# Loads of y and of the token-block tasks on GpSimd's queue, and other turns for the second pair's tasks

## The chip, the cores and the metric

The kernel runs on 1 core of one Trainium2 chip. The metric is device time in microseconds (us) of one execution; the time given for a kernel is the median of its runs. All tensors are float32. Matrix products are made from float32r operands (a float32 value split in a high and a low part, `split` below), three products for each pair of operands (`mm3`).

Engines by the profile's names: PE is TensorE (matmuls), DVE is VectorE, ACT is ScalarE, POOL is GpSimd, SP is SyncE, which here only issues DMA transfers. SPq and POOLq are the instruction queues of SP and GpSimd. Each engine works through its own list of instructions in order and stands at an instruction until the semaphores that it waits for have come; what is behind it in the list waits too.

## The reference

`x` is 2048 tokens of 640 features. It is normalized, and three things are added up: `x`, the real part of a two-dimensional discrete Fourier transform of the normalized `x`, and a gated MLP of it.

```python
def _A_ref(x, dft_seq_re, dft_seq_im, dft_hid_re, dft_hid_im):
    a = jnp.einsum("bsd,ed->bse", x, dft_hid_re)
    b = jnp.einsum("bsd,ed->bse", x, dft_hid_im)
    return jnp.einsum("ts,bse->bte", dft_seq_re, a) - jnp.einsum("ts,bse->bte", dft_seq_im, b)

def _B_ref(x, W_gate, W_up, W_down):
    gate = jnp.einsum("bsd,df->bsf", x, W_gate)
    up = jnp.einsum("bsd,df->bsf", x, W_up)
    gate = gate * (gate > 0)
    return jnp.einsum("bsf,fd->bsd", gate * up, W_down)

xn = _layernorm(x, axis=-1)
return x + _A_ref(xn, ...) + _B_ref(xn, ...)
```

The sizes: S = 2048 tokens, D = 640, F = 1728. The products are made in a Strassen-like scheme (blocks B11, B12, B21, B22 and their sums T1 to T4), so sums of blocks are prepared on VectorE ahead of the matmuls.

## The kernel before

**Two phases.** Phase 1 makes the Fourier part. It works on four chunks `c` of 512 token columns (CH). For each chunk, tiles of the sequence DFT matrices (128 x 1024, 512 KB) are loaded (L482, L564: `raw` and `tk`), combined on VectorE (L560), split by ScalarE (L105) and VectorE (L106) into a ring of three tiles `cb`, and multiplied with the normalized tokens. `raw` has five buffers, and a load that needs one waits until VectorE has finished with it. Then five `hidden` units for each half m = 1 and m = 0 multiply by the hidden DFT (weights `in_hid`, loaded in L657, split into `wu`), and their result is added to `y` (L671). The two `y` buffers hold 5 x 512 columns each; a chunk's y is loaded from the transposed x in `hidden`'s `load` (L655, the residual `x`), and, for chunks 0 and 1, stored to the DRAM tensor `y_early` one unit after the last addition (L674, GpSimd). The next chunk's L655 writes the same buffer, so it waits until L674 has landed.

Phase 2 makes the MLP for two pairs of chunks, q = 1 first (chunks 2 and 3), then q = 0. A unit `gate_up(q, f)` (f = 0 to 12, plus a rest) loads and splits gate and up weights (L785, `z`, `gw`) and makes 54 matmuls with ScalarE and VectorE copies between them (L820 `p`, L823 `oa`, L825 `u`, L829, L831, L832, L836, L839, L840), and leaves `h`. After units 1, 3, 5, 7, 9, 11 and 12 a unit `down` multiplies two `h` by W_down (weights L766, `wdt`) and adds to `y` (L910).

**Token-block tasks.** The MLP needs the normalized tokens transposed, in the blocks of the scheme. For each pair q six tasks (`token_sets`, steps 0 to 5) make them: load the rows of mean and reciprocal deviation, broadcast to all partitions (L300 or L317, from `rows`), and a block of the transposed x (L301 or L318, from `in_xt`), into two buffers `st` called `mr` and `a` or `ab`; normalize and combine in place on VectorE (`make`: L304 and L305 for steps 0 and 1; L323, L324 and L327 for steps 2 to 5); store to the DRAM tensor `set` on GpSimd (L307, or two stores in L336). Steps 2 to 5 have four loads each (two L317, two L318), steps 0 and 1 three (two L300, one L301). Each task's loads write the two buffers that the task before has used, so they wait until its stores have landed. The sets are loaded again in L629 (`load_set`, SP) and split into `xs_early` and `sets_b`, the operands of the MLP.

Pair 1's tasks run in phase 1, from chunk 0's V3 on, 14 units or more apart (SPACE): `make` six units after the load, the store eight units after. Pair 0's tasks run in phase 2 while q = 1 is computed: a task is a unit of its own in front of `gate_up(1, f)` for the f in SET_TURNS, its `make` comes one unit and its store two units after the load. At f = 11 the first finished set of pair 0 (B12) is loaded (`load_set_now`); the scheduler puts that load and its copies into the lists as early as it believes the data to be there.

**What sets the order.** The list `todo` holds units with four steps: load, prepare, run, finish. `drive` goes through them with loads four units (phase 1) or two units (phase 2) ahead of the run; `defer` places makes and stores a number of units later. From this the tile framework's scheduler makes one list for each engine. In the kernel before, all loads stand in SP's list: DFT tiles, hid weights, y, rows, in_xt, sets, z, W_down. GpSimd's list has the stores to `first`, `set`, `y_early` and little else.

Of the kernel before, what the change touches and what calls it, by code (L numbers as in the profile page):

```python
# [12 lines left out]
P = 128  # L13
S, D, F = 2048, 640, 1728
KD = D // P
CH = 512
W2 = 2 * CH
HC = CH // 2
# [28 lines left out]
def fnet_reglu_kernel(  # L47
# [15 lines left out]
    nc = tc.nc  # L63
# [31 lines left out]
    def bank():  # L95
        return psum_p.tile([P, CH], F32, name="ps")

    def stage():
        return stages[-1].tile([P, W2], F32, name="st")
# [4 lines left out]
    def split(hi, lo, src):  # L104
        nc.scalar.activation(hi, src, AF.Copy)  # L105
        return nc.vector.tensor_tensor(lo, src, hi.bitcast(F32), op=OP.subtract)  # L106

    def mm3(ps, w, m, first, last, more=False):

        (wh, wl), (mh, ml) = w, m  # L110
        nc.tensor.matmul(ps, wh, mh, start=first, stop=False, skip_group_check=more)  # L111
        nc.tensor.matmul(ps, wh, ml, start=False, stop=False, skip_group_check=more)  # L112
        nc.tensor.matmul(ps, wl, mh, start=False, stop=last, skip_group_check=more)  # L113
# [6 lines left out]
    def defer(units, f):  # L120

        deferred.setdefault(now[0] + units, []).append(f)
# [155 lines left out]
    def token_sets(q, step, stage=stage, distance=(6, 8)):  # L278

        ch = xt[:, q * W2 : (q + 1) * W2].rearrange("(k p) t -> k p t", p=P)  # L280
        st_r = rows[:, q * W2 : (q + 1) * W2]
        tt = nc.vector.tensor_tensor
        part = lambda st, i: st[:, i * CH : (i + 1) * CH]
        t = {}

        def unit(load, make, keep):
            def begin():
                load()
                defer(distance[0], make)
                defer(distance[1], keep)  # L290

            todo.append((begin, idle, idle, idle))

        if step < 2:
            cs = slice(step * CH, (step + 1) * CH)

            def load():
                t["mr"], t["a"] = stage(), stage()[:, :CH]
                for i in range(2):
                    nc.sync.dma_start(part(t["mr"], i), st_r[i : i + 1, cs].to_broadcast([P, CH]))  # L300
                nc.sync.dma_start(t["a"], ch[4][:, cs])  # L301

            def make():
                tc.keep_in_program_order(tt(t["a"], t["a"], part(t["mr"], 0), op=OP.add))  # L304
                tt(t["a"], t["a"], part(t["mr"], 1), op=OP.mult)  # L305

            unit(load, make, lambda: nc.gpsimd.dma_start(sets[q][X4][:, cs], t["a"]))  # L307
            return

        k, hs = (step - 2) // 2, (step - 2) % 2 * HC  # L310
        hs = slice(hs, hs + HC)
        cols = lambda ap: ap.rearrange("p (c t) -> p c t", c=2)

        def load():
            t["mr"], t["ab"] = stage(), stage()
            for i in range(2):
                nc.sync.dma_start(cols(part(t["mr"], i)), cols(st_r[i : i + 1])[:, :, hs].to_broadcast([P, 2, HC]))  # L317
                nc.sync.dma_start(cols(part(t["ab"], i)), cols(ch[k + 2 * i])[:, :, hs])  # L318

        def make():  # L320
            mr, ab = t["mr"], t["ab"]
            for i in range(2):
                tc.keep_in_program_order(tt(part(ab, i), part(ab, i), part(mr, 0), op=OP.add))  # L323
                tt(part(ab, i), part(ab, i), part(mr, 1), op=OP.mult)  # L324

            (a0, a1, b0, b1), (t1, t2, t3, t4) = ([st[:, i * HC : (i + 1) * HC] for i in range(4)] for st in (ab, mr))
            sub = lambda o, i0, i1: tt(o, i0, i1, op=OP.subtract)  # L327
            sub(t1, a1, a0)
            sub(t2, b1, t1)
            sub(t3, b1, a1)  # L330
            sub(t4, b0, t2)

        def keep_sets():
            cs = slice(k * CH + hs.start, k * CH + hs.stop)
            for i, st in ((B11, t["ab"]), (T1, t["mr"])):
                nc.gpsimd.dma_start(sets[q][i : i + 4, :, cs].rearrange("i p t -> p i t"),  # L336
                                  st.rearrange("p (i t) -> p i t", i=4))

        unit(load, make, keep_sets)
# [15 lines left out]
    def raw():  # L355
        return raw_p.tile([P, W2], F32, name="raw")
# [280 lines left out]
    def load_set_now(q, blocks):  # L637
        for i in blocks:
            for step in load_set(q, [i]):
                step()  # L640

    def y_chunk(half, e):
        return Y[half][:, e]

    def hidden(c, m, e):
        t = {}
        half = int(c == NCHUNK - 1)
        y = lambda: y_chunk(half, e)
        first = m == 1

        def load():
            if first:
                if (c, e) == (NCHUNK - 1, 0):
                    Y[1] = get_right()
                nc.sync.dma_start(y(), xt[e * P : (e + 1) * P, c * CH : (c + 1) * CH])  # L655
            t["s"] = raw()[:, :D]
            nc.sync.dma_start(t["s"], hid[m, e])  # L657

        def prepare():
            t["w"] = w = wring.tile([P, 2, D], F32R, name="wu")  # L660
            split(w[:, 0], w[:, 1], t["s"])

        def run():
            ps = bank()
            for i, d in enumerate((0, 1, 4, 2, 3)):
                mm3(ps, (t["w"][:, 0, d * P : (d + 1) * P], t["w"][:, 1, d * P : (d + 1) * P]),
                    PQ[c, m, d], i == 0, i == KD - 1)
            t["ps"] = ps

        def finish():  # L670
            nc.vector.tensor_tensor(y(), t["ps"], y(), op=OP.add)  # L671
            if not first and c < 2:
                b = c * CH
                defer(1, lambda: nc.gpsimd.dma_start(y_early[:, e, b : b + CH], y()))  # L674

        todo.append((load, prepare, run, finish))

    def drive(far, ahead, pinned=None):
# [237 lines left out]
        todo.append((idle, prepare, run, idle))  # L916

    load_set_now(1, SETS_B)
    SET_TURNS = [1, 2, 4, 6, 8, 9]
    for q in (1, 0):  # L920
        gate_up_rest(q)
        fs = [NF]
        for f in range(NF):
            if q == 1 and f in SET_TURNS:
                token_sets(0, SET_TURNS.index(f), lambda: pool("stage3").tile([P, W2], F32, name="st"), (1, 2))
            gate_up(q, f)
# [43 lines left out]
```

## Time and profile before

| what | value |
|---|---|
| median of 3 runs | 1078.13 us (1075.41 to 1082.65) |
| the profiled execution: time | 1079.5 us |
| the profiled execution: span from first to last instruction | 1077.7 us |
| mean granted TensorE clock in it | 0.995 |
| busy ACT / POOL | 402.3 us (37%) / 33.0 us (3%) |
| DMA moved, over the span | 164.52 MB, mean 153 GB/s |
| GpSimd's own transfers (software_dynamic queue) | 19.40 MB, 4.6% of the DMA engines' span |

Transfers that the change and the prediction speak of, from the list of DMA issues: what and where to, who issues, how many, size, median time from issue to landing.

| transfer | queue | count | KB each | us to landing |
|---|---|---|---|---|
| raw<-in_dft | SP | 94 | 512 | 4.3 |
| y<-in_xt (L655) | SP | 20 | 256 | 4.5 |
| st<-rows (L300, L317) | SP | 24 | 256 | 4.7 |
| st<-in_xt (L301, L318) | SP | 20 | 256 | 3.3 |
| st<-set (L629) | SP | 18 | 512 | 3.8 |
| out<-y | SP | 20 | 256 | 3.0 |
| set<-st (L336) | GpSimd | 16 | 512 | 5.6 |
| y_early<-y (L674) | GpSimd | 10 | 256 | 4.1 |

How to read it: the span is covered by the engine that is busy nearly all of it, so the interesting numbers are the places where that engine is idle, and what released it there. A transfer's time to landing counts from its issue to the semaphore of its last byte. A row of waits names the waiting engine and line, what released it, the microseconds in total, how often, and the longest. A row of the chain of waits names a start, a length and the work that the next piece waited for. In a row of the timeline, start and length are followed by engine, line, operation, operands and count; the bracket is idle time before, and what ended it.

### The profile page before, as it was taken

How to read it: one execution, taken by the hardware profiler on the slowest of the kernel's cores; microseconds unless marked ns; L12 is line 12 of the kernel's file. 1: busy time of each engine (PE TensorE's matmuls, PEld its weight loads, DVE VectorE, ACT ScalarE, POOL GpSimd, SP SyncE). 2: the span in 40 equal slices, each digit the busy share in tenths (PEclk: the TensorE clock that was granted, in tenths of full speed). 3: DMA queues.
4: the chain of work that ended last, by engine and by line, in shares of the span. 5: the costliest groups of instructions: out<-in, count | busy, mean ns of one | idle time of the engine just before them, and what ended most of it. 6: DMA issues, size and time to landing. Idle time of an engine off the chain costs nothing.

```text
span 1077.7 us, 12192 instructions
## 1 busy us (share of the span) xinstructions
PE 1059.7 (98%) x4660; PEld 872.1 (81%) x4660; DVE 784.7 (73%) x1085; ACT 402.3 (37%) x506; POOL 33.0 (3%) x51
## 2 busy tenths in 40 slices
PE   8999999999989999999999999999999999999998
PEld 6888888878778887888888888877888888888886
DVE  7946986875689488668588778677569865685654
ACT  5744453432333233344352422322244433233211
POOL 2100000000000000000000000010000000000000
PEclk9999999999999999999999999999999999999999
DMA  8974654666477567435462232343039211111002
GB/s 307 347 249 162 234 176 142 230 227 215 170 236 240 191 213 263 164 122 183 149 200 99 96 127 86 104 138 113 26 112 323 80 59 52 49 50 49 25 1 98
DMA packets 60410, 164.52 MB, mean 153 GB/s; under 512 B 8128, under 2 KB 16320, under 8 KB 60352
## 3 DMA queue, kind: packets, MB, share of 16 engines
q1 hardware_dynamic: 55456, 144.35, 40.8%
q0 software_dynamic: 4896, 19.40, 4.6%
q8 instruction: 36, 0.59, 0.2%
q14 instruction: 22, 0.18, 0.1%
HBM read 139.07 MB, written 23.61 MB: 151 GB/s over the span
## 4 chain that ended last, share of the span: by engine, by line
PE 68%; issue 18%; DVE 7%; DMA 5%; ACT 1%; POOL 0%; SPq 0%; POOLq 0%; DVEq 0%; ACTq 0%
PE ps L111 22%; PE ps L113 22%; PE ps L112 22%; DMA raw<-in_dft 2%; DMA set<-st 1%; DVE cb L106 1%; PE ps L907 1%; DVE y L910 1%; DMA st<-set 1%; DVE raw L560 1%; DMA st<-in_wd 1%; DMA y<-in_x 0%; DVE st L327 0%; DVE st L324 0%; DVE xs_early L106 0%
## 5 line engine op out<-in xcount | busy, mean ns | idle before, releaser
L105 ACT ACTIVATE cb<-raw 128x1024 fp32r<-128x1024 f32 x78 | 82.1, 1056 | 121.6 <-PE ps L113 102.3
L106 DVE TENSOR_TENSOR cb<-raw,cb 128x1024 fp32r<-128x1024 f32 x78 | 94.9, 1220 | 44.5 <-ACT cb L105 41.2
L910 DVE TENSOR_TENSOR y<-ps,y 128x512 f32<-128x512 f32 x140 | 91.1, 687 | 17.5 <-PE ps L113 16.8
L112 PE MATMUL ps<-cb,xs_late 128*128 128x512 f32 x256 | 100.5, 393 | 2.7 <-DVE cb L106 2.7
L112 PE MATMUL ps<-h,wdt 128*128 128x512 f32 x260 | 101.3, 389 | 0.0
L111 PE MATMUL ps<-xs_early,gw 128*128 128x512 f32 x260 | 101.1, 389 | 0.0
L113 PE MATMUL ps<-h,wdt 128*128 128x512 f32 x260 | 101.1, 389 | 0.0
L112 PE MATMUL ps<-xs_early,gw 128*128 128x512 f32 x260 | 101.1, 389 | 0.0
L113 PE MATMUL ps<-xs_early,gw 128*128 128x512 f32 x260 | 101.1, 389 | 0.0
L111 PE MATMUL ps<-h,wdt 128*128 128x512 f32 x260 | 100.3, 390 | 0.0
L111 PE MATMUL ps<-cb,xs_late 128*128 128x512 f32 x256 | 100.2, 392 | 0.0
L113 PE MATMUL ps<-cb,xs_late 128*128 128x512 f32 x256 | 100.2, 391 | 0.0
L111 PE MATMUL ps<-cb,xs_early 128*128 128x512 f32 x244 | 96.0, 394 | 2.3 <-ACT xs_early L102 2.3
L112 PE MATMUL ps<-cb,xs_early 128*128 128x512 f32 x244 | 95.5, 391 | 0.0
L113 PE MATMUL ps<-cb,xs_early 128*128 128x512 f32 x244 | 95.0, 390 | 0.0
L111 PE MATMUL ps<-sets_b,gw 128*128 128x512 f32 x208 | 81.9, 394 | 2.8 <-ACT u L825 2.8
L112 PE MATMUL ps<-sets_b,gw 128*128 128x512 f32 x208 | 81.5, 392 | 0.0
L113 PE MATMUL ps<-sets_b,gw 128*128 128x512 f32 x208 | 81.3, 391 | 0.0
L113 PE MATMUL ps<-pqt,wu 128*128 128x512 f32 x200 | 78.3, 392 | 2.5 <-DVE wu L106 2.4
L105 ACT ACTIVATE gw<-z 128x2176 fp32r<-128x2176 f32 x26 | 52.7, 2026 | 74.9 <-PE ps L113 63.0
L111 PE MATMUL ps<-pqt,wu 128*128 128x512 f32 x200 | 78.0, 390 | 1.3 <-ACT wu L105 1.3
L112 PE MATMUL ps<-pqt,wu 128*128 128x512 f32 x200 | 77.9, 389 | 0.0
(151 smaller groups left out, 1963.7 us busy)
## 6 DMA issues: line engine op xcount, KB each, us to landing
raw<-in_dft SPq DMA_DIRECT2D x94, 512.0 KB, 4.3
z<-in_wgu SPq DMA_DIRECT2D x26, 640.0 KB, 3.9
raw<-in_hid SPq DMA_DIRECT2D x40, 320.0 KB, 3.9
st<-set SPq DMA_DIRECT2D x18, 512.0 KB, 3.8
st<-in_wd SPq DMA_DIRECT2D x26, 320.0 KB, 3.5
tk<-in_dft SPq DMA_DIRECT2D x16, 512.0 KB, 4.4
set<-st POOLq DMA_DIRECT2D x16, 512.0 KB, 5.6
st<-rows SPq DMA_DIRECT2D x24, 256.0 KB, 4.7
```

Of the source, the lines that this page charges most:

```text
L105: nc.scalar.activation(hi, src, AF.Copy)
L106: return nc.vector.tensor_tensor(lo, src, hi.bitcast(F32), op=OP.subtract)
L111: nc.tensor.matmul(ps, wh, mh, start=first, stop=False, skip_group_check=more)
L112: nc.tensor.matmul(ps, wh, ml, start=False, stop=False, skip_group_check=more)
L113: nc.tensor.matmul(ps, wl, mh, start=False, stop=last, skip_group_check=more)
L560: sub = lambda o, i0, i1: nc.vector.tensor_tensor(o, i0, i1, op=OP.subtract)
L907: nc.tensor.matmul(ps, w[:, v, es], h[:, 0, cs], start=i == 0 and v == 0, stop=end and v == 1)
L910: nc.vector.tensor_tensor(y, ps, y, op=OP.add)
```

## The change

20 loads of y (L655), 24 of rows (L300, L317) and 20 of in_xt (L301, L318) are issued by `nc.gpsimd.dma_start` instead of `nc.sync.dma_start`; nothing else is different in them. SET_TURNS, the units of the MLP in front of which pair 0's tasks stand, is 1, 2, 4, 5, 7, 8 instead of 1, 2, 4, 6, 8, 9.

```diff
@@ -297,8 +297,8 @@
             def load():
                 t["mr"], t["a"] = stage(), stage()[:, :CH]
                 for i in range(2):
-                    nc.sync.dma_start(part(t["mr"], i), st_r[i : i + 1, cs].to_broadcast([P, CH]))
-                nc.sync.dma_start(t["a"], ch[4][:, cs])
+                    nc.gpsimd.dma_start(part(t["mr"], i), st_r[i : i + 1, cs].to_broadcast([P, CH]))
+                nc.gpsimd.dma_start(t["a"], ch[4][:, cs])
 
             def make():
                 tc.keep_in_program_order(tt(t["a"], t["a"], part(t["mr"], 0), op=OP.add))
@@ -314,8 +314,8 @@
         def load():
             t["mr"], t["ab"] = stage(), stage()
             for i in range(2):
-                nc.sync.dma_start(cols(part(t["mr"], i)), cols(st_r[i : i + 1])[:, :, hs].to_broadcast([P, 2, HC]))
-                nc.sync.dma_start(cols(part(t["ab"], i)), cols(ch[k + 2 * i])[:, :, hs])
+                nc.gpsimd.dma_start(cols(part(t["mr"], i)), cols(st_r[i : i + 1])[:, :, hs].to_broadcast([P, 2, HC]))
+                nc.gpsimd.dma_start(cols(part(t["ab"], i)), cols(ch[k + 2 * i])[:, :, hs])
 
         def make():
             mr, ab = t["mr"], t["ab"]
@@ -652,7 +652,7 @@
             if first:
                 if (c, e) == (NCHUNK - 1, 0):
                     Y[1] = get_right()
-                nc.sync.dma_start(y(), xt[e * P : (e + 1) * P, c * CH : (c + 1) * CH])
+                nc.gpsimd.dma_start(y(), xt[e * P : (e + 1) * P, c * CH : (c + 1) * CH])
             t["s"] = raw()[:, :D]
             nc.sync.dma_start(t["s"], hid[m, e])
 
@@ -916,7 +916,7 @@
         todo.append((idle, prepare, run, idle))
 
     load_set_now(1, SETS_B)
-    SET_TURNS = [1, 2, 4, 6, 8, 9]
+    SET_TURNS = [1, 2, 4, 5, 7, 8]
     for q in (1, 0):
         gate_up_rest(q)
         fs = [NF]
```

In the lists that the scheduler makes of it, TensorE's is unchanged. SP's loses the 64 loads and keeps the others in their order but for one W_down and one z load near unit 9, which change places. In phase 1 two neighbouring tiles change places in VectorE's and ScalarE's lists at three points. In GpSimd's list each y load of chunks 1 and 2 stands right behind the y_early store of the same part of the buffer, and a task's loads stand behind the stores of the task before, in the order L317, L317, L318, L318. On VectorE the four long makes of pair 0 stand at the end of unit 3, in unit 4, at the end of unit 5 and at the end of unit 7 (before: at the end of units 3, 5 and 7, and in unit 8). ScalarE's and VectorE's copies of the first loaded set to xs_early stand in unit 8 instead of unit 9, on ScalarE behind L825 instead of ahead of it.

## The prediction

> **What bounds the kernel now.** I read the busy shares first, then the windows around the stretches where TensorE is not full, then the chain of waits through two of them, then SP's waits and GpSimd's issues there.
>
> ```profile
> PE 1059.7 (98%) x4660; PEld 872.1 (81%) x4660; DVE 784.7 (73%) x1085; ACT 402.3 (37%) x506; POOL 33.0 (3%) x51
> ```
>
> TensorE is the bound: 18.0 us of the 1077.7 us span are not busy. 4.3 us of that lie in the first 20 us and 4.4 after the last matmul, both untouched here. The other 9.3 are six places; four of them by windows of 10 us (length, then busy time and count of PE, PEld, DVE, ACT, POOL; granted clock; DMA share; GB/s):
>
> ```profile
> 290.00:300.00 10.00, 7.33 (x29) 5.41 (x28) 7.28 (x10) 4.51 (x6) 0.00 (x0) 0.92 0.68 239
> 300.00:310.00 10.00, 10.00 (x42) 8.19 (x41) 10.00 (x18) 2.93 (x4) 0.76 (x1) 0.91 0.57 180
> 320.00:330.00 10.00, 8.10 (x36) 6.33 (x35) 8.85 (x12) 4.27 (x6) 0.00 (x0) 1.00 0.79 256
> 410.00:420.00 10.00, 8.66 (x39) 6.87 (x38) 5.88 (x8) 3.29 (x5) 0.00 (x0) 1.00 0.83 280
> 720.00:730.00 10.00, 7.48 (x31) 5.84 (x30) 9.67 (x12) 4.74 (x6) 1.28 (x2) 0.92 0.71 242
> ```
>
> The reader is to see three prices of a pause. The idle time is ten less the busy time. Refilling costs about 0.26 more: around the pause of 2.67 us two neighbouring matmuls start 3.05 us apart instead of 0.227 (2.82 lost), and the next one 0.11 late. After the idles of 2.67 and 2.52 the clock reads 0.92 and 0.91 for two windows, (0.08 + 0.09) x 10 = 1.7 us; after 1.90 it stays at 1.00. So the pauses cost: near 294, 2.67 + 0.26 + 1.7 = 4.6; near 321, 1.90 + 0.26 = 2.2; near 216 (window 210 to 220, busy 9.49), 0.51 + 0.26 = 0.8; near 418, two pauses (420 to 430 busy 9.88), 1.34 + 0.12 + 0.52 = 2.0; near 726, 2.52 + 0.26 + 1.7 = 4.5; near 827 (820 to 830, busy 9.76), 0.24 + 0.26 = 0.5. Together 14.6 us: no change of waits can gain more.
>
> The chain of waits before the pause at 294 (start, length, what):
>
> ```profile
> 256.90 7.08 DMA set<-st
> ...
> 264.00 0.37 SPq L318
> ...
> 264.48 4.70 DMA raw<-in_dft
> ```
>
> A token-block store takes 7.08 us to land; SP stands at the next task's load (L318), because that load writes the stored buffer; the DFT tile queued behind it leaves 0.5 us later, and VectorE's L560 (269.26) waits for it. SP's own waits from 238 to 324:
>
> ```profile
> SPq L655 <- DMA y_early<-y: 19.9, 5, 8.7
> ...
> SPq L318 <- DMA set<-st: 9.2, 2, 5.9
> ...
> SPq L317 <- DMA set<-st: 4.6, 1, 4.6
> ```
>
> In 86 us, 33.7 us of SP go to waits for GpSimd's stores, with the DFT loads behind them. VectorE's waits for DFT tiles there sum to 25.7 us. TensorE lived on its ring of three tiles until 294.
>
> **The change, part by part.** 64 loads move from SP to GpSimd: 20 of y, 24 of rows, 20 of in_xt. Left behind on SP are DFT, weight and set loads in their old order. SP is freed of 64 issues and of its waits at L655, L317, L318, L300, L301 (146 us over the span, most of them off the path). What this is worth is what the pauses cost:
> - Near 294: the whole 4.6. The loads behind SP's 33.7 us then leave when VectorE frees a slot.
> - Near 321: VectorE is busy without a break from 297 to 313 catching up, so slots come free late (the tile that ends this pause is issued at 313.44). Without that backlog most goes; but the place repeats in every chunk (0.8 near 216, 2.0 near 418), so I leave 0.7: gain 1.5, bounds 0 and 2.2.
> - Near 216: SP waits for slots, not for tokens, from 200 on; gain 0.3, bounds 0 and 0.8.
> - Near 418: the load SP stands at is a set load (L629, issued 415.57 when the store of 409.12 has landed), which stays on SP. Gain 0, bounds 0 and 2.0.
> - Near 827: start of the second pair's MLP, untouched.
>
> GpSimd gets 64 issues. Its own rows say 0.55 us for a plain tile (L674) and 0.76 for one in pieces (L336): 32 x 0.55 + 32 x 0.76 = 42 us on an engine busy 33 of 1077.7. The new waits sit in its queue: each y load waits for the y_early store just before it (4.1 us median to landing), with the next y_early and set stores behind it. Those stores' data come 8 to 13 us apart (344.78, 352.82, 363.79, 373.72, 386.44), so 0.55 + 4.1 + 0.55 fits. The first y loads stand ahead of the first sa store (42.93), waiting for LayerNorm on that buffer; SP issued them at 52.35, and sa is next written at 70.72. Token loads of the first pair have 36 us or more from the buffer's release to their first use (264 to 298, 319.57 to 346, 359 to 401). All these I cost at nothing; the cover is that slack.
>
> The turns: with 1, 2, 4, 6, 8, 9 the steps at 8 and 9 follow closely. The chain of waits there:
>
> ```profile
> 706.77 6.58 DMA set<-st
> 713.35 2.98 issue
> 716.33 0.10 DVE st L323
> ...
> 727.78 0.59 ACT u L825
> ```
>
> The last task's make stands in VectorE's list within unit 8, 4.94 us late (716.33 instead of 711.39); its store lands at 722.9, the finished set is loaded from 722.95 to 726.80, and that holds ScalarE's copy to xs_early, which stands ahead of u L825, for which TensorE waits. With 1, 2, 4, 5, 7, 8 the last make moves to the end of unit 7, the place that the make at 699.23 has, and its first store is in DRAM at 706.5. In the changed program's list the copy stands one unit earlier, behind unit 8's u (711.72) instead of unit 9's p. The load takes 3.9 us, at most the 6.6 of a contended one: data by 710.5 to 713.2, where a late copy holds L829 (713.70) by 0.6 at most, with 15 matmuls (3.4 us) to spare. Gain 4.5.
>
> What is late next: the close pair is now at units 4 and 5, and the make of the second stands in VectorE's list inside unit 4, as it stood in unit 8. The same 4.94 us there moves ScalarE's h to 724.54 and u to 725.60 on the old clock; TensorE runs dry at 725.90, u ends at 726.20: 0.3 us, as no set copy stands between. GpSimd makes it earlier or later. A 256 KB store lands in 4.1 us from GpSimd and 3.0 from SP, so +1.1, +0.76 for an issue, and one more 0.76 if the second rows load must wait: +2.6. But the store itself lands in 3.2 us (703.32 to 706.53) when no SP load leaves beside it, against 6.58: -3.4. I take +0, 0.3 us, the row it copies; bounds 0 and 0.3 + 2.6 + 0.26 + 1.7 = 4.9.
>
> Could GpSimd's queue hold itself up? Its rows (start, length, then idle before):
>
> ```profile
> 348.49 0.75 POOL L336 DMA_DIRECT2D set<-st  x1 [3.16 <-DVE st L327]
> 352.07 0.76 POOL L336 DMA_DIRECT2D set<-st  x1 [2.82 <-DVE cb L106]
> 352.82 0.55 POOL L674 DMA_DIRECT2D y_early<-y  x1
> ```
>
> The second set store waits until the first has landed, here as in all eight pairs (3.4 us apart at least), though its data were ready; the small y_early store goes at once behind a set store still in flight. So a large transfer waits for room and small ones do not. A load in pieces lies between.
>
> Sum: -4.6 - 1.5 - 0.3 - 4.5 + 0.3 = -10.6. The profiled execution took 1079.5 us (span 1077.7 and 1.8 around it), so 1068.9; it is 1.4 over the median of 1078.13, so **1067.5** as a median.
>
> **Rivals.** A is the forecast, 0.43: with its small terms 1066 to 1070, on both sides of 1067.35, which is 1% under the median (1% is what a measurement here can tell from none).
> B: VectorE gains a lead of 2 us, and the pauses near 216, 321 and 418 go too: 4.6 + 2.2 + 0.8 + 2.0 + 4.5 = 14.1, 1064.0. For: 418's tile came 4.0 us late only. Against: SP still stands at L629. 0.29.
> C: the pair at 4 and 5 pauses at its upper bound: -10.9 + 4.9 = -6.0, 1072. 0.11.
> D, slower: GpSimd lets no transfer start before the last has landed. Then the four loads at unit 4 end 4 x 5.6 (the set store's median) after 713.35, at 735.8, 19.4 us later than 716.33: a pause of 0.3 + 19.4 + 2.0 = 21.7; the next task needs 6 x 5.6 = 33.6 us where about 25 lie between the makes' places in the list (645 to 670), 8.6 + 2.0 more. -10.9 + 32.3 = +21.4, 1099.5. It loses from 8.6 us of lateness at unit 4 on. For: the set pairs above; against: L674 at 352.82. 0.11.
> E: nothing comes of the loads, since the 16 DMA engines and not SP's queue set when tiles land, and the make in unit 4 costs what that in unit 8 did: 1078. Against: DMA share 0.54 from 240 to 290. 0.03. The Trainium skill (DMA: Bandwidth & Descriptors, "Issuing engines are not separate DMA queues") says that issuing from several engines only saves the sequencer's issue time; by that rule this case holds, and SP's waits above speak against it.
> F: each GpSimd issue waits out a VectorE instruction, at the longest that of L106 to gw (2.42 us). Three loads stand ahead of the first make op, 7.3 us later: a pause of 0.3 + 7.3 + 2.0, -10.9 + 9.6 = -1.3, 1077. Against: 16 set stores took 752 to 771 ns each with VectorE 73% busy. 0.03. The Trainium skill (SBUF — State Buffer, "SBUF: two separate sides") warns that VectorE in a two-port mode keeps GpSimd from writing descriptors; the trace's even issues disagree for this kernel.
>
> **How the numbers follow.** Faster by over 1%: half of A (0.22) and B, 0.51. Within 1%: the rest of A (0.21), C, E, F: 0.38. Slower: D, 0.11. The range runs from 1062 (B, less 2 for the scatter of the runs, 1075.41 to 1082.65) to 1074.5 (C and its scatter); it leaves out D, E and F, 0.17.
>
> **What would show it.** Right: windows 290 to 310 full at clock 1.00; no SP wait on set<-st or y_early<-y but at L629; the window of 720 full; a short pause near 418 still there. Wrong: VectorE's L323 waiting over 8 us for loads in unit 4, GpSimd's L317 and L318 several us apart, or issues there of over 1 us.

## The result, and the profile after

| | median | runs | ratio to before, 95% interval |
|---|---|---|---|
| before, measured again beside it | 1082.14 us (1075.41 to 1087.18) | 20 | |
| after | 1075.16 us (1069.41 to 1079.26) | 20 | 0.9931 [0.9913, 0.9948] |

The change makes the kernel 0.69% faster, 7.5 us on 1082.14 (5.6 to 9.4); the medians lie 7.0 apart. Forecast were 10.6 us and a time of 1067.5. Of the 7.7 us between 1067.5 and 1075.16, 4.0 are the base: three runs of the kernel before had a median of 1078.13, twenty have 1082.14. The other 3.7 are the sum. One execution of a kernel below, the first with added copies, took 1785.85 us at a granted clock of 0.557, and neither it nor its trace stands in any number here.

The profiled execution after took 1079.26 us (span 1077.1), the longest of its 20, so its span is no measure of the change; its places are. Its windows (length, then busy time and count of PE, PEld, DVE, ACT, POOL; granted clock; DMA share; GB/s):

```profile
290.00:300.00 10.00, 10.00 (x46) 8.29 (x45) 9.14 (x11) 4.95 (x6) 0.00 (x0) 1.00 0.69 222
300.00:310.00 10.00, 10.00 (x45) 8.02 (x44) 8.79 (x15) 3.10 (x5) 1.51 (x2) 1.00 0.63 197
310.00:320.00 10.00, 6.79 (x30) 5.04 (x28) 4.95 (x6) 1.91 (x3) 2.90 (x5) 0.99 0.83 284
320.00:330.00 10.00, 8.77 (x27) 7.05 (x28) 8.34 (x12) 4.28 (x6) 0.00 (x0) 0.66 0.70 228
410.00:420.00 10.00, 9.50 (x42) 7.51 (x41) 5.64 (x8) 2.80 (x4) 0.77 (x1) 1.00 0.76 250
420.00:430.00 10.00, 8.64 (x30) 6.65 (x31) 8.70 (x11) 3.61 (x5) 0.00 (x0) 0.83 0.77 266
...
720.00:730.00 10.00, 10.00 (x46) 8.29 (x45) 6.62 (x6) 4.66 (x5) 0.00 (x0) 1.00 0.21 73
...
820.00:830.00 10.00, 8.93 (x39) 6.74 (x38) 8.29 (x11) 7.82 (x11) 0.00 (x0) 1.00 1.02 349
```

The pauses near 294 and 726 are gone: both windows are full, at clock 1.00. The pause that lay near 321 lies near 316, and is 4.44 us instead of 1.90; behind it the clock is at half speed for 6.83 us, which costs 3.4. Near 418 there is a pause as before, of 1.73 us instead of 1.34, and here the clock falls behind it for 3.41 us, another 1.7. Near 827 there are two, of 0.57 and 0.50 us, instead of one of 0.24. The chain of waits through the pause near 316 (start, length, what):

```profile
309.33 1.24 DVE cb L106
310.58 8.61 DMA raw<-in_dft
319.25 1.11 issue
320.36 0.83 DVE wu L106
321.23 0.79 PE ps L113
```

The last matmul before the pause and the first behind it (start, length, instruction, idle before):

```profile
316.40 0.39 PE L112 MATMUL ps<-pqt,wu 128*128 128x512 f32 x1
321.23 0.79 PE L113 MATMUL ps<-pqt,wu 128*128 128x512 f32 x1 [4.44 <-DVE wu L106]
```

It hangs on one DFT tile: issued at 310.58, when VectorE had freed its buffer, in place 8.61 us later, while the median of its kind is 4.3. The same place in the kernel before, its chain and then its window, neither of which the prediction showed:

```profile
313.44 7.29 DMA raw<-in_dft
```

```profile
310.00:320.00 10.00, 10.00 (x45) 8.28 (x45) 5.80 (x6) 3.60 (x4) 0.77 (x1) 1.00 0.98 325
```

There too the tile took 7.29 us, in a stretch where the DMA engines were busy to 0.98. What is in flight beside it after the change, from GpSimd's timeline (start, length, instruction, idle before):

```profile
305.41 0.77 POOL L336 DMA_DIRECT2D set<-st  x1 [18.08 <-DVE st L327]
309.26 0.76 POOL L336 DMA_DIRECT2D set<-st  x1 [3.08 <-issue]
310.02 0.71 POOL L317 DMA_DIRECT2D st<-rows  x1
315.67 0.74 POOL L317 DMA_DIRECT2D st<-rows  x1 [4.94 <-issue]
```

These are a 512 KB store at 309.26 and a 256 KB load at 310.02; SP issues the tile itself at 310.58 and two more loads at 311.72 and 313.05. SP does what the prediction said: none of its waits from 238 to 324 names a store any more, and over the whole span only L629 still waits for a token-block store (14.2 us). Its longest waits from 238 to 324:

```profile
SPq L564 <- DVE cb L106: 34.4, 7, 14.6
SPq L657 <- DVE cb L106: 13.6, 5, 5.7
SPq L564 <- DVE wu L106: 9.2, 4, 6.6
```

### The profile page after: what moved, and what is told of

It reads as the page before. It is cut to its first block, busy times and chain, and to the rows that moved or that the text cites. A ratio compares the mean times of both kernels' runs of the same rounds, so it can differ in the third digit from the quotient of the medians.

```text
span 1077.1 us, 12197 instructions
## 1 busy us (share of the span) xinstructions
PE 1060.8 (98%) x4660; PEld 873.3 (81%) x4660; DVE 786.8 (73%) x1085; ACT 402.5 (37%) x506; POOL 73.8 (7%) x115
## 4 chain that ended last, share of the span: by engine, by line
PE 85%; DVE 6%; DMA 5%; ACT 2%; issue 1%; SPq 0%; DVEq 0%; ACTq 0%
PE ps L113 28%; PE ps L111 28%; PE ps L112 28%; DMA raw<-in_dft 3%; DVE cb L106 1%; DMA raw<-in_hid 1%; PE ps L907 1%; DVE raw L560 1%; DMA st<-in_wd 1%; ACT cb L105 0%; DMA y<-in_x 0%; DVE y L910 0%; DVE wu L106 0%; DVE pqt L351 0%; DVE sb L451 0%
## 5 line engine op out<-in xcount | busy, mean ns | idle before, releaser
L113 PE MATMUL ps<-pqt,wu 128*128 128x512 f32 x200 | 80.0, 400 | 5.2 <-DVE wu L106 5.1
L111 PE MATMUL ps<-pqt,wu 128*128 128x512 f32 x200 | 79.6, 398 | 1.7 <-ACT wu L105 1.7
L112 PE MATMUL ps<-pqt,wu 128*128 128x512 f32 x200 | 79.4, 397 | 0.0
```

## The experiments

Two questions were open: which part of the change does what, and why the pause near 316 grew. For the second, theory B (backlog) says that VectorE, without a break from 294 to 314, frees the buffer late (the backlog is the work that VectorE still has to catch up with); theory C (contention) that the tile lands late because GpSimd's transfers share the DMA engines with it.

**The loads alone, the turns alone.** Each is half of the diff shown above.

```diff
-    SET_TURNS = [1, 2, 4, 5, 7, 8]
+    SET_TURNS = [1, 2, 4, 6, 8, 9]
```

> Only the first part of the change: 64 loads on GpSimd's queue, the old turns 1, 2, 4, 6, 8, 9. Theory S (the two parts act apart): the pause near 294 is gone, the one near 316 to 321 is as long as in the changed kernel (4.4 us and 3.4 at a lower clock), and the pause near 726 (2.5 us, 0.26 to refill, 1.7 at a lower clock: 4.5) stays. The changed kernel is 0.0069 x 1082 = 7.5 us below the kernel before; without the 4.5 it is about 3.0 us, a ratio of 0.997. Rival L (the loads do it all, since GpSimd also frees SP for the load of the finished set): no pause near 726, a ratio of 0.993.

> Only the second part: turns 1, 2, 4, 5, 7, 8, all loads on SP as before. Theory S: the pause near 726 is gone, those near 294 (2.7 us) and 321 (1.9 us) stay as they were; 4.5 us below the kernel before, a ratio of 0.996. Rival L: the pause near 726 stays or comes back elsewhere in the MLP, a ratio of 0.999 to 1.001.

Loads alone: 0.9948 [0.9927, 0.997]; the pause near 294 is gone, that near 316 is 2.67 us, that near 724 is 2.06. The time lies between the two forecasts, 0.997 and 0.993, and decides nothing; the pause near 724 stays, as theory S said. In phase 1 VectorE's list is that of the changed kernel (read from 285 to 322), so 2.67 and 4.44 us come of the same work: the pause differs that much from one execution to the next.

Turns alone: 0.9992 [0.9974, 1.001]. There the pause near 726 is gone, as theory S said, but others have come in the MLP, as its rival said, and the time is the rival's; windows, and the chain of waits ahead of the largest:

```profile
640.00:650.00 10.00, 9.83 (x44) 7.82 (x42) 9.30 (x16) 3.63 (x4) 1.51 (x2) 1.00 0.52 168
660.00:670.00 10.00, 8.74 (x39) 6.96 (x38) 9.67 (x14) 3.09 (x2) 0.00 (x0) 1.00 0.10 19
710.00:720.00 10.00, 9.91 (x43) 7.61 (x41) 8.46 (x18) 2.60 (x5) 1.17 (x2) 1.00 0.46 164
```

```profile
647.58 5.99 DMA set<-st
654.53 5.67 DMA z<-in_wgu
...
667.92 1.14 DVE h L106
669.06 1.20 DVE y L910 x2
```

SP stands at the fifth task's x loads (L318, issued at 653.59) until the set store of 647.58 has landed; the MLP's weights (z) leave only behind them, at 654.53, and VectorE's work comes late. Idle times of 0.64, 1.26 and 0.38 us, with 0.26 each to refill, are 3.1 of the 4.5 us gained. By their times the parts could still act apart (5.6 and 0.9 us, and 7.5 for both); it is the traces that show that they don't. The three pauses are missing in the changed kernel and come back with only the y loads moved (0.36, 1.27 and 0.29 us): the new turns pay best when the token loads no longer stand ahead of the weights.

**Either half of the loads.** L655 back on SP; then the other way round, L300, L301, L317 and L318 on SP and only L655 on GpSimd. Both have the new turns.

```diff
-                nc.gpsimd.dma_start(y(), xt[...])
+                nc.sync.dma_start(y(), xt[...])
```

> The changed kernel with the 20 loads of y back on SP (only the 44 token-block loads on GpSimd). Theory T (the chain of waits: the DFT tile ahead of the pause near 294 stood behind a token load, L318): the pause near 294 is gone or under 0.7 us, that near 316 is 3 to 5 us; ratio 0.993. Theory Y (SP's waits for y_early, 19.9 us of its 33.7 in that stretch, are as bad): a pause of 1.5 us or more near 294, ratio 0.995 to 0.998.

> Only the 20 loads of y on GpSimd, token-block loads on SP, new turns. With the token loads alone on GpSimd the pause near 294 was gone and the ratio 0.9933. Theory T (the token loads were what held the DFT tiles): the pause near 294 stays, 1.5 to 2.7 us; ratio 0.998 to 1.001. Rival Y (either part frees enough of SP's 33.7 us of waits): no pause over 0.7 us near 294; ratio 0.993 to 0.996.

Token loads alone: 0.9933 [0.9907, 0.9958]. Loads of y alone: 0.9927 [0.9906, 0.9947]. In both the window 290 to 300 is full, and the pause near 316 is 2.96 and 3.06 us. The window with only y moved:

```profile
290.00:300.00 10.00, 10.00 (x46) 8.29 (x45) 9.72 (x13) 5.59 (x7) 0.00 (x0) 1.00 0.66 209
```

Theory T falls: either half gives the whole, as far as the intervals can tell. With only y moved, SP still waits 18.3 us for set stores in 238 to 324 (23.5 for y_early with only tokens moved, 33.7 for both before):

```profile
SPq L318 <- DMA set<-st: 10.2, 2, 6.1
...
SPq L317 <- DMA set<-st: 8.1, 2, 7.9
```

The wait of the chain at 264 is still there (a set store of 7.23 us, and SP at L318 until 262.54), and no pause follows it; that TensorE's ring of three tiles now outlasts it is a reading of that.

**One store less beside the tile.**

```diff
-            for i, st in ((B11, t["ab"]), (T1, t["mr"])):
+            for i, st, cs in [(B11, t["ab"], cs)] + [(T1, t["mr"], cs)] * ((q, step) != (1, 3)) + ...
```

> The changed kernel, with the second 512 KB store of the task made at 296 to 307 (issued at 309.26) not made there but with the next task's stores, about 40 us later (it then stores the next task's data, so one block of tokens is not the reference's). VectorE's and ScalarE's lists, and SP's, are those of the changed kernel. Theory C (contention: the DFT tile issued at 310.58 lands at 319.19, 8.6 us later, because the store, the loads of rows behind it and five SP loads are in flight together): with 512 KB less the tile lands 1.8 us sooner or more (512 KB at 284 GB/s), and the rows loads leave 3 us sooner and are out of its way: the pause near 316 shrinks from 4.4 us to 1.5 us or less and the lower clock behind it (3.4 us) goes at least in part; 4 to 6 us below the changed kernel, a ratio to before of 0.988 to 0.990. Theory B (backlog: the tile is issued late because VectorE works without a break from 294 to 314): tile issued at 310.6 as before, pause 3.5 to 4.4 us, ratio 0.993.

The kernel leaves out one 512 KB store. 0.993 [0.9909, 0.9951]. Chain of waits:

```profile
308.04 8.42 DMA raw<-in_dft
```

The tile took as long, and the pause is 3.13 us. The ratio is the one given for B, but this does not decide for B, since the load was not less: with the store gone, the next task's 1 MB of loads moved up to 304.89, 306.58, 307.30 and 311.19, around the tile. The expectation had them "out of its way", which was wrong.

**The whole task three units later.** `{3: 3, 2: -3}` moves the fourth task's place and leaves the others.

```diff
-                free[0] = len(todo) + SPACE
+                free[0] = len(todo) + SPACE + {3: 3, 2: -3}.get(len(steps), 0)
```

> The changed kernel, with the fourth token-block task of the first pair three units later (load, VectorE's make and stores; the other five tasks where they were). VectorE's eight instructions of the make leave the stretch 295 to 307 and stand some 20 us later, and the stores and next loads go with them. Theory B (backlog) and theory C (contention) both make the pause near 316 go (4.4 us, 0.26 to refill, up to 3.4 at a lower clock): 5 to 8 us below the changed kernel, a ratio to before of 0.986 to 0.989. Theory M (a pause of this kind only moves on, to where the make now stands): a new pause of 2 us or more between 320 and 350, ratio 0.991 to 0.994.

0.9881 [0.986, 0.9902], median 1069.30 us: faster than both kernels. No pause near 316 (windows), with the tile of the chain of waits landing in half the time:

```profile
300.00:310.00 10.00, 10.00 (x46) 8.29 (x45) 7.49 (x9) 3.51 (x4) 0.00 (x0) 1.00 0.69 219
310.00:320.00 10.00, 9.94 (x44) 7.92 (x43) 8.76 (x14) 3.55 (x5) 0.71 (x1) 1.00 0.55 172
```

```profile
306.79 4.34 DMA raw<-in_dft
```

It moved VectorE's work and the transfers together, so B and C both stood. Theory M falls: no new pause of more than 0.2 us up to 400.

**Transfers added beside the tile.** To that kernel three DRAM copies of 512 KB on GpSimd's queue are added, first released by the first wu tile, then by the second.

```diff
+        go = nc.gpsimd.tensor_tensor(mark, wf, wf, op=OP.mult)
+        with tc.issue_after(go.ins):
+            for i in range(3):
+                nc.gpsimd.dma_start(junk[i], xt[0:P, 0:W2])
```

> The kernel with the fourth task three units later (0.9881 of before, no pause near 316; its DFT tile issued at 306.79 landed after 4.4 us), and added to it three copies of 512 KB from DRAM to DRAM on GpSimd's queue, released when the first wu tile of those units is ready (near 301) and so in flight at 302 to 312. No engine's list of arithmetic changes but one instruction of one column on GpSimd. Theory C (the pause near 316 of the changed kernel comes from transfers of GpSimd's queue in flight beside the tile): the tile of 307 lands after 6.5 to 9 us and the pause is back, 1 to 4 us without the lower clock; ratio 0.990 to 0.993. Theory B (VectorE's backlog alone): landing at most 5.5 us, no pause over 0.7 us, ratio 0.988.

> The kernel with three added copies of 512 KB once more (ratio 0.9919 against 0.9881 without them), for a profile at full clock: its landing times. Theory C: the DFT tile issued near 307 lands after 6.5 to 9 us (4.4 without the copies) and TensorE pauses 1 to 4 us near 315. Theory B: at most 5.5 us, no pause over 0.7 us, and the 4 us of time lie elsewhere.

> The kernel with the fourth task three units later and three added DRAM copies of 512 KB on GpSimd's queue, now released by the second wu tile (ready at 301.2), not the first: the earlier copies had moved at 296 to 302, before the tile in question was issued at 307.4, and it landed after 4.5 us. Now they move at 303 to 311. Theory C (contention): the tile issued near 307 lands after 6.5 us or more and TensorE pauses 1 to 4 us near 315. Theory B (backlog): it lands within 5.5 us, pause under 0.7 us.

Released by the first tile, run twice: 0.9919 [0.9888, 0.995] and 0.9901 [0.9876, 0.9926]. The second run's trace shows the copies' packets at 295 to 303, before the tile, which landed in 4.55 us with a pause of 0.64 us behind it; by the letter of the expectation this was B, but the load had missed its place. Released by the second tile (0.9921 [0.9894, 0.9947]) the packets lie at 303 to 310, and the chain of waits and the window read:

```profile
305.70 7.24 DMA raw<-in_dft
```

```profile
310.00:320.00 10.00, 7.79 (x33) 5.83 (x32) 6.42 (x9) 2.31 (x3) 0.00 (x0) 1.00 0.55 200
```

With VectorE's list unchanged, GpSimd's transfers alone bring the landing from 4.34 to 7.24 us and pauses of 1.58 and 0.64 us back. That is theory C: transfers can do it. Three copies are more than what the changed kernel has in flight there, so it says nothing of how much.

**Transfers taken away, VectorE's work left.** The changed kernel, the fourth task's make in its place, its stores left out there and the fifth task's loads held.

```diff
+    if (c, m, e) == (1, 1, 3):
+        late["go"] = nc.gpsimd.tensor_tensor(mark, wf, wf, op=OP.mult).ins
...
+                behind_each(held and late["go"], tc, lambda: nc.gpsimd.dma_start(...))
```

> The changed kernel with VectorE's make of the fourth task where it was (295 to 307) and no transfer of GpSimd's queue between 305 and 316: both of that task's stores are left out there (the next task's stores write their place too, so those tokens are not the reference's), and the fifth task's loads stand behind a GpSimd instruction that waits for the fourth wu tile (near 316 to 320), its make four units later. VectorE's, ScalarE's and SP's lists are the changed kernel's until 340. Theory C: the DFT tile issued near 308 to 310 lands within 5.5 us instead of 8.6 and the pause near 316 is under 1.2 us (4.4 before). Theory B: issued as late, the pause is 2.5 us or more.

Chain of waits and window:

```profile
307.71 4.87 DMA raw<-in_dft
...
313.74 0.83 DVE wu L106
```

```profile
310.00:320.00 10.00, 9.29 (x42) 7.31 (x41) 6.99 (x9) 4.39 (x7) 2.37 (x4) 1.00 0.75 255
```

The last matmul before the pause and the first behind it:

```profile
313.52 0.39 PE L112 MATMUL ps<-pqt,wu 128*128 128x512 f32 x1
314.62 0.50 PE L113 MATMUL ps<-pqt,wu 128*128 128x512 f32 x1 [0.71 <-DVE wu L106]
```

The tile lands in 4.87 us and the pause is 0.71. How long TensorE still had work when the tile was issued can be put beside it: the last matmul before the pause started 5.82 us after the issue in the changed kernel and 5.81 here. The landing is 3.74 us shorter, the pause 3.73. So contention is what 3.73 of the 4.44 us hang on, with VectorE's work in its place; what is left for theory B is at most the 0.71. (The time, 0.9909 [0.9885, 0.9933], says less: with the delayed tasks the pause near 411 is 3.27 us.)

**More room for GpSimd's descriptors.**

```diff
-    nc = bacc.Bacc(..., dynamic_dma_scratch_size=1024)
+    nc = bacc.Bacc(..., dynamic_dma_scratch_size=2048)
```

> The changed kernel with twice the scratch memory for the descriptors of GpSimd's queue (2048 bytes of each partition instead of 1024), nothing else. Theory R (the second of two 512 KB stores is held because the queue has no room for its descriptors until the first has drained): the second set store and the loads behind it start at once, 0.8 us after the first instead of 3.5 to 3.9, in all eight pairs. For the time: the pause near 316 then meets the same transfers bunched 3 us sooner, 3 to 5 us long, ratio 0.992 to 0.994. Theory W (something else orders them, such as a semaphore): still 3.5 us apart.

0.9929 [0.9904, 0.9954]. GpSimd's timeline:

```profile
302.63 0.77 POOL L336 DMA_DIRECT2D set<-st  x1 [17.61 <-DVE st L327]
304.67 0.76 POOL L336 DMA_DIRECT2D set<-st  x1 [1.28 <-DVE st L327]
306.37 1.44 POOL L317 DMA_DIRECT2D st<-rows  x2 [0.93 <-DMA set<-st]
```

The second store now waits only for its own data (VectorE's L327), 2.0 us behind the first instead of 3.9 (1.9 to 2.7 in all eight pairs), and the loads behind it for the store whose buffer they write. So room it was, as theory R said; the 0.8 us of the expectation overlooked the data. The time stays: the tile beside it took 8.66 us, the pause is 3.21.

**Three more moves.** To the kernel with the fourth task three units later: the five loads of the finished set (L629) on GpSimd as well; then, without these, the sixth task four units earlier. Last, the fourth task's move and the new turns without the change of queue.

```diff
+                todo.append(load_set(1, [early_sets.pop(0)], queue=nc.gpsimd))
...
+                free[0] = len(todo) + SPACE + {3: 3, 2: -3, 1: -4}.get(len(steps), 0)
```

> The kernel with the fourth task three units later, and also the five loads of the finished set of the first pair (L629, 512 KB each) issued by GpSimd's queue. Theory Q (near 411 the DFT tiles come late since SP stands at the second of these loads until the set store has landed): the pause of 1.3 us near 411 goes, 1.5 us below the kernel without this edit, ratio 0.9865. Theory C (the tile issued at 403 lands 6.3 us later because the set store, the set load and SP's tiles are in flight together, whatever queue issues them): the pause stays at 1 us or more, ratio 0.988 to 0.990.

> The kernel with the fourth task three units later, and the sixth task four units earlier: its make moves from 392 to 399 to about 375 to 382, its 1 MB of stores from 398 to 405 to about 384 to 391. Theory C (the pause near 411 comes from the set stores, the set loads behind them and the DFT tiles in flight together): the tile issued near 403 lands in under 5 us and the pause of 1.3 us near 411 is under 0.4; ratio 0.9865. Rival M (VectorE is 7 us fuller near 378 and the lateness only moves): a new pause of over 0.5 us between 385 and 400, or the same one near 411, ratio 0.988 to 0.990.

> The kernel before (all loads on SP) with the new turns and with the fourth task three units later: what moving the one task is worth without the change of queue. Theory S (SP's waits for the stores are a cause of their own): SP stands at the fourth task's loads until the third's stores have landed, DFT tiles come late near 270 to 295, and a pause of 1 us or more stays there; ratio 0.994 to 0.998. Rival N (only the place of the task counts, not the queue): no pause over 0.7 us before 400; ratio 0.988 to 0.990.

Sets too: 0.9882 [0.9857, 0.9906], pause near 409 of 0.94 us for 1.30; no gain that can be told, and neither theory Q (the pause goes) nor C (1 us or more) is met. Sixth task earlier: 0.9887 [0.9867, 0.9906], rival M: the pause near 411 is gone and one of 1.90 and 0.76 us stands near 397 (windows):

```profile
390.00:400.00 10.00, 8.10 (x36) 6.31 (x34) 4.58 (x6) 2.83 (x4) 0.53 (x1) 1.00 0.65 192
410.00:420.00 10.00, 10.00 (x46) 8.29 (x45) 8.49 (x9) 4.56 (x5) 0.00 (x0) 1.00 0.67 217
```

Task moved with the loads on SP: 1.0022 [1.0006, 1.0038], slower than before by 0.06 to 0.38%, with pauses of 3.48, 2.50 and 2.54 us near 297, 377 and 424 (windows, then SP's waits from 330 to 430):

```profile
290.00:300.00 10.00, 7.62 (x33) 5.65 (x31) 6.36 (x10) 4.09 (x6) 0.00 (x0) 1.00 0.50 180
370.00:380.00 10.00, 7.50 (x33) 5.92 (x33) 4.38 (x5) 1.70 (x2) 0.56 (x1) 1.00 0.61 210
```

```profile
SPq L655 <- DMA y_early<-y: 18.7, 4, 7.6
SPq L318 <- DMA set<-st: 13.5, 2, 7.1
```

Theory S, and beyond its numbers: the move that is worth 5 us on the changed kernel costs 2 to 3 with SP's queue as it was. The queue is a cause of its own.

## Why the prediction was wrong

The direction held, and so did the places of the two large terms; one term had the wrong sign, and most of the miss in the sum is made of it. Every sign that the prediction gave for being right came (290 to 310 full, no store but at L629, 720 full, a short pause near 418), and the time was missed all the same: none of the signs looked at 310 to 320.

- **Near 294, −4.6: right.** The window is full in every kernel with loads moved. That both kinds of load had to go was not so: either half is enough.
- **Near 726, −4.5: the pause went, as forecast;** its price is less sure. With the loads moved and the old turns it was 2.06 us and cost no clock, 2.3 in that trace, and the ratios with new and old turns (0.9931 and 0.9948) overlap. With the loads on SP 3.1 of it come back, the cost of the pair at units 4 and 5; the forecast had put 0.3 on that and had not asked what stands behind the token loads in SP's list. In the changed kernel VectorE's L323 of unit 4 waits 4.0 us (the bound given was 8) and no pause follows; with only tokens moved there is one of 0.82 us.
- **Near 321, −1.5 (bounds −2.2 and 0): the step that failed.** The prediction read the tile's issue at 313.44 and blamed VectorE's backlog ("Without that backlog most goes"). It did not read the landing of 7.29 us in the same chain, nor the window's DMA share of 0.98, and it costed the transfers of the new queue by their issues and waits, with nothing for their bytes beside the tile. The bookkeeping of the place is plain: in eight traces the pause is the landing, plus 1.64 us of VectorE and TensorE, less the time from the issue to the last matmul before it. Before: 7.29 + 1.64 − 7.04 = 1.89, and 1.90 is measured. After: 8.61 + 1.64 − 5.82 = 4.43, and 4.44 is measured. Taking the pause at 294 away brought TensorE there 4.1 us earlier but the issue only 2.9, and the store and the load nearer to the tile (1.32 and 0.56 us ahead of it, for 1.57 and 1.92). So of the 2.54 us by which the pause grew in this profile, 1.32 are the landing and 1.22 the issue, which did not follow TensorE; that second part is not contention. In the five other traces named below the landing takes 7.60 to 8.66, and its growth is the larger part in four. With its clock the place costs 4.44 + 0.26 + 3.4 = 8.1 in this profile, and 2.67 to 3.21, 0.26 and 1.7, so 4.6 to 5.2, in five others with all or some of the loads moved and the fourth task in its place (loads alone, either half, one store less, more room): 2.4 to 5.9 worse than the 2.2 before. With +2.8, the mean of the five, for −1.5 the sum is −6.3, a gain inside the measured 5.6 to 9.4. That it comes out so well is partly luck, since the other terms are single executions too: the clock near 418 or the price near 726 moves it by 2 us.
- **Near 418, 0 of 2.0: right in place;** 1.73 us here, with the clock 3.7 in all, and 0.77 to 1.85 in the five related kernels. SP still stands at L629 there, up to 5.0 us. That L629 is its cause is not shown: on GpSimd's queue it left 0.94.
- **Near 216, −0.3:** 0.63 us after, 0.51 before, and none in some; not to be told. Near 827, left out as untouched: 1.07 us after for 0.24 before, and 0.20 to 0.49 in the five; not explained.
- **The clock's price of a pause** ("after 1.90 it stays at 1.00") was no rule: after 1.73 near 419 the clock fell; the last section has what the traces show of it.
- **The slack of the token loads,** "36 us or more", is 34, 26.4 and 42 us by the three places that the prediction names. No pause hangs on it.
- **The base.** The profiled execution of before, 1079.5, was taken to lie 1.4 above the median; it lies 2.6 below that of 20 runs. The range took in three runs' scatter, not the scatter of their median.

The rivals: B (all pauses go) and C (unit 4) did not come. D (one transfer at a time) did not come as a time. Its mechanism, room, is confirmed for large transfers, and one of the prediction's signs of being wrong came: GpSimd's two L317 near 316 are 5.65 us apart. No pause is shown to hang on that; with more room the two go together and the pause near 316 is still 3.21, while the one near 418 was 0.77 us, for 1.26 to 1.85 in the five without (the four named above and the changed kernel), one execution each. E falls with the loads alone at 0.9948. Its mechanism, though, is what the place near 316 shows: the tile landed after 4.87 us without GpSimd's transfers beside it and after 8.61 with them. The Trainium skill (DMA: Bandwidth & Descriptors, "Issuing engines are not separate DMA queues") says that transfers of all issuing engines interleave on the same 16 DMA engines. These two landings agree. The same section of the Trainium skill says that another issuing engine only saves issue time. SP's waits for stores, 33.7 us before and none after from 238 to 324, and the pause near 294 that went with them, do not agree. F falls: GpSimd's issues in 305 to 319 took 0.71 to 0.77 us each.

## What to carry to other kernels

When a pause is removed, the next wait must be worked out for the engine's new, earlier time: write for each later place when the data is issued, how long it takes to land in that stretch, and when it is needed, and read the DMA share there before blaming the engine that issues late. Moving loads off a queue that stands at other transfers' waits helped here, but the bytes stay. Where the DMA engines are busy (0.98 and 0.83 in the window of this pause), transfers may have to move in time: one task moved three units, its transfers and its VectorE work together, gave 5 us. And a sum of a few microseconds needs a base from more than three runs.

## What the runs showed of the hardware

The clock falls by a grid. In every trace with more than one half-speed stretch these start whole multiples of 3.413 us apart (before: 18.42, 298.31 and 728.39, which is 82 and 126 steps), whatever the pause. Behind the first 20 us, how much idle time lies inside one step separates all the cases: 1.72, 1.73, 1.78, 1.85 us and more were each followed by a step at half speed, which costs 1.7; 1.50 and less, in a step at full speed, by none. In the first 20 us it does not: ahead of the pause near 18.5, steps with 1.68, 1.72 and 1.94 us idle (no traffic, tokens only, copies later) were followed by full speed, and only 2.12 and more by half (the grid is drawn back from each trace's later stretches). Why is open. (In the profile after, a step already at half speed with 1.33 us idle was followed by another; hence the 3.4.) A pause of 2.06 us (loads alone, near 724), cut by the grid into 1.31 and 0.75, cost no clock, and one of 1.73 in a single step did. The 1.90 near 321 before, cut into 1.34 and 0.57, cost none either. By these figures two executions of one kernel can differ by 1.7 us for each pause from 1.7 to 3.0 us (twice 1.50), an estimate. The Trainium skill (TensorE: Matmul & The Clock Gate, "Part 1: The HAM clock gate") says that activity is judged in free-running windows of 3413 ns. The steps here agree. About half a window of idle time was enough here.

GpSimd's queue holds a second 512 KB store until there is room for its descriptors: in the pair near 305 it goes 3.9 us after the first with 1024 bytes of scratch, and 2.0 with 2048, where it waits only for its data.
